# Three chunks per relayout, an earlier w_in and filled TensorE gaps in the first batch of a fused attention and feed-forward kernel

## The chip, the cores and the metric

The kernel runs on one core of a Trainium2 chip. The time is the device time of one execution in microseconds (us). The engines are TensorE (PE; its weight loads are listed apart as PEld), VectorE (DVE), ScalarE (ACT), GpSimd (POOL) and SyncE (SP). SP issues transfers inside the chip and stores, POOL issues the loads that cast float32 to bf16. [...] Results of TensorE are in PSUM, eight banks of 128 x 512 float32.

## The reference

Talking-heads attention followed by a feed-forward part with a squared ReLU, for 8 batches, 12 heads, 448 tokens and head size 64:

```python
scores = scale * np.matmul(q, k.transpose(0, 1, 3, 2))
scores = np.einsum('bhij,hg->bgij', scores, w_pre)
attn = np.exp(scores - np.max(scores, axis=-1, keepdims=True))
attn = attn / (np.sum(attn, axis=-1, keepdims=True) + 1e-09)
attn = np.einsum('bhij,hg->bgij', attn, w_post)
x = np.matmul(attn, v).transpose(0, 2, 1, 3).reshape(B * S, H * D)   # 3584 x 768
h = np.maximum(x @ w_in, 0.0)                                        # 3584 x 2048
out = h * h @ w_out                                                  # 3584 x 768
```

The mixing of heads (w_pre) stands between the scores and the softmax, so all 12 heads of a token have to meet before the maximum is taken.

## The kernel before, in words

**Attention of one batch.** The 448 tokens are four blocks: the last 64 tokens (block r=0, "tail", two heads at a time in 128 rows) and three blocks of 128 rows (r=1 to 3). For each block `score` (L460) multiplies q with k per head (L472), and VectorE or ScalarE copies the result to `snat`, where a row is a query and the heads lie one behind another. There are two `snat` buffers, used in turn by the blocks. Then the layout is changed: `relayout` (L504, its transfer in `move`, L499) takes ten queries of all 12 heads to 120 partitions of a buffer `sch` or `schl`, one row of 448 keys per query and head. That is a chunk. A batch has 45 of them: 6 for r=0 and 13 for each other block, the first of the 13 being made of leftovers of two blocks.

**A chunk** (`chunk`, L552): one product with a 120x120 matrix `wmix` mixes the heads (L564), VectorE takes the minimum (the sign is turned, L569), ScalarE the exponential with its sum (L572), VectorE the reciprocal (L578), POOL scales the second mixing matrix with it into `wq` (L581), four products (L588) give the mixed and transposed weights, and VectorE or ScalarE copies them to `atb` (L302, L304 are the copies of both engines). After 20 chunks `av` (L613, products L624) multiplies half 0 (192 queries) with v, and after the last chunk half 1 (256 queries); the results go to `xt`.

**The feed-forward part** takes two batches together (896 columns) in units of 128, 256, 256 and 256 columns (`UNITS`, `unit`, L649): 96 products with w_in (L669), ReLU on ScalarE (L682), square on POOL (L685), products with w_out (L701), a copy on VectorE (L716) and stores. A unit needs `xt` of its columns; every product of L669 waits for all of w_in, and L701 for w_out.

**The order of the work.** A planner (`Planner`, L76) runs once while the kernel is built. Each operation has an engine, an assumed duration, dependencies, a priority and the PSUM banks it takes. The planner plays the work in time, takes on every engine the ready operation of best priority, and the order that comes out is the fixed order of the instructions on each engine. Chunk n has priority n, its relayout n - 7 (`AHEAD`), FFN work 1e6 and more, so it fills what the attention leaves.

**Loads.** POOL first issues k, the tails of q and q of batch 0, then v. w_in follows in six loads behind the `wq` of chunks 0, 1, 2, 4, 6 and 8 (L776, pieces of 1024 bytes of float32), q and k of batch 1 behind chunks 11 and 14, w_out in four loads behind chunks 17, 20, 23 and 26 (L815). At most seven are under way.

Of the kernel before, what the change touches and what calls it, by code (L numbers as in the profile page):

```python
# [42 lines left out]
AHEAD = 7  # L43
# [4 lines left out]
GROUP = 2  # L48
SLACK = {"PE": 200, "SP": 800, "POOL": 100}
MOST = {"m": 3, "a": 2, "f": 2, "g": 6, "mix": 7}  # L50
PLACES = [[0, 128, 256, 384], [64, 192, 320, 0]]
# [9 lines left out]
UNITS = [(0, 128), (128, 384), (384, 640), (640, 896)]  # L61


class Op:
    def __init__(self, engs, lat, pri, fn, deps, bank, frees, mode):
        self.engs, self.lat, self.pri, self.fn = engs, lat, pri, fn
        self.bank = bank if isinstance(bank, list) else [bank] if bank is not None else []
        self.frees, self.mode = frees, mode
        self.left, self.next, self.at, self.eng, self.ns = 0, [], None, None, 0
        for d in deps:  # L70
            if d is not None:
                self.left += 1
                d.next.append(self)


class Planner:  # L76
# [3 lines left out]
    def __init__(self):  # L80
        self.ops = []
        self.banks, self.most = [], {}

    def add(self, eng, ns, pri, fn, deps=(), lat=60, bank=None, frees=None, mode=0):
        op = Op(eng if isinstance(eng, dict) else {eng: ns}, lat, pri, fn, list(deps), bank, frees, mode)
        self.ops.append(op)
        return op

    def run(self):
# [22 lines left out]
        t, mode = 0, 0  # L112
        while True:
            for eng, heap in ready.items():
                if busy[eng] > t:
                    continue
# [25 lines left out]
                else:  # L142
                    item = None
                    if first is not None:
                        kept.remove(first)
                        item, op, args = first, first[2], []
                if item is not None:
# [21 lines left out]
            while events and events[0][0] == t:  # L169
                op = heapq.heappop(events)[2]  # L170
                if op is None:
                    continue
                if isinstance(op, tuple):
# [14 lines left out]
        assert len(order) == len(self.ops)  # L188
# [4 lines left out]
def kernel(  # L193
# [62 lines left out]

    ident = sb.tile([P, P], BF16, name="ident")
    nc.vector.memset(qt[:, :, :], 0.0)
    for x in range(2):
        load_tail(0, x)  # L260
    for h0 in range(0, H, 4):
        load_kv(ks, k, 0, h0, h0 + 4)
        if h0 == 0:
            masks.make_identity(nc, ident[:, :])
    for h0 in range(0, H, 4):
        load_q(0, h0, h0 + 4)
# [32 lines left out]

    def copy(eng, out_, in_):  # L300
# [20 lines left out]
    def load(nbytes, pri, fn, deps):  # L321
        if len(loads) >= 7:
            deps = list(deps) + [loads[-7]]
        op = add("POOL", 700, pri, fn, deps)
        done = add("LOAD", nbytes / 230.0, len(loads), lambda: None, [op], lat=6000)
# [3 lines left out]
    q_in, k_in, v_in = {}, {}, {}  # L329
    score_ops, scopy = {}, {}  # L330
# [12 lines left out]
    def t_qk(b, p):  # L343
# [27 lines left out]
        at = p - 5 if b == 0 else pri + 3  # L371
# [4 lines left out]
    def t_tail(b, g):  # L376
# [14 lines left out]
        pri = b * NCHUNK - 19 + 3 * g  # L391
# [68 lines left out]
    def score(b, r, p):  # L460
        sn = snat[(b * (NJ + 1) + r) % 2]
        tag = "mfa"[p % 3] if b == 0 and r == 0 else "g"
        group = [p] if r == 0 else range(p, p + GROUP)
        keys = [(tag, "s", b, r, p_, x) for p_ in group for x in range(1 if r == 0 else 2)]

        def mms(*got):
            for key, slot in zip(keys, got):
                _, _, _, _, p_, x = key
# [5 lines left out]
        pri = b * NCHUNK + C0[r] - AHEAD - 0.6 - (0.7 if r == 0 else 1.4) * (NPAIR - p)  # L474
        n = b * (NJ + 1) + r - 2
        old = list(relay_of[n]) if n >= 0 else []
# [15 lines left out]
    ring, side, src_of = [], {}, {}  # L492

# [4 lines left out]
    def move(n, pri, ns, deps, outs, srcs, lat):  # L498
        op = add("SP", ns, pri, lambda: nc.sync.dma_start(out=outs, in_=srcs), deps)  # L499
        done = add("DMA", ns / 2, pri, lambda: None, [op], lat=lat)  # L500
# [3 lines left out]
    def relayout(b, c):  # L504
        r, cc = block_of(c)
        n = b * NCHUNK + c
        blk = b * (NJ + 1) + r
        sn, sn0 = snat[blk % 2], snat[(blk - 1) % 2]
        lat = 5500 if b == 0 and c else 4500
        here = relay_of.setdefault(blk, [])  # L510
        deps = list(scopy[b, r])
        pri = n - AHEAD
        if r == 2 and cc == 0:
            src_of[n] = schl
            here.append(move(n, pri, 700, deps + side.get(b - 1, []), schl[24:96, :], sn[120:126, :, :], lat))
            return
# [12 lines left out]
        for of, r0, r1, srcs in parts:  # L529
            ns = 770 if r1 - r0 > 90 else 500  # L530
            relay_of[of].append(move(n, pri, ns, deps + old, src_of[n][r0:r1, :], srcs, lat))
        if r == 0 and cc == 5:
            here.append(move(
                b * NCHUNK + C0[2], pri + 0.5, 500, deps + side.get(b - 1, []),
# [3 lines left out]
    def places(b, c):  # L538
        r, cc = block_of(c)
        rest, first = (0, NS) if b % 2 else (P_ROWS, 0)  # L540
        if r == 0:
            return [(0, rest + CI * cc, 0, CI)]
# [9 lines left out]
    def chunk(b, c):  # L552
        n = b * NCHUNK + c
# [8 lines left out]

        def f_m(slot):
            nc.tensor.matmul(  # L564
# [30 lines left out]
        def f_ac(eng):  # L595
            for half, x0, s0, w in where:
                copy(
                    eng, atb[half][:, :, :, x0:x0 + w].rearrange("p j g m -> p (j g) m"),
# [3 lines left out]
        m = m_op[n] = add("PE", 190, n, keep(mk, f_m), relay[n] + [at_op.get(n - NE), w_ready], lat=200, bank=mk)  # L602
# [6 lines left out]
        old = [av_op[b - 1, half, g] for half in {u[0] for u in where} for g in range(3)] if b > 0 else []  # L609
# [3 lines left out]
    def av(b, half, g):  # L613
        nx = (XA, XB)[half]
        to = spans(b % 2, half)
        key = ("g", "v", b, half, g)

        def mms(slot):
            v_ = slot[:, :].rearrange("p (a c) -> p a c", a=2)
            for i in range(2):  # L620
                c2 = 2 * g + i
                for jb in range(NB):
                    for hh in range(2):
                        nc.tensor.matmul(  # L624
                            v_[64 * hh:64 * hh + 64, i, 0:nx],
                            lhsT=vs[:, 2 * c2 + hh, jb, :],
                            rhs=atb[half][:, jb, 2 * c2 + hh, :],
# [3 lines left out]
        def evac():  # L631
            v_ = slots[key][:, :].rearrange("p (a c) -> p a c", a=2)
            for c0, x0, w in to:
                nc.scalar.copy(out=xt[:, 2 * g:2 * g + 2, x0:x0 + w], in_=v_[:, :, c0:c0 + w])

        n0 = b * NCHUNK
        cs = range(n0, n0 + C0[2] + 1) if half == 0 else range(n0 + C0[2], n0 + NCHUNK)
        old = []
        if b >= 2:
            for ui, (a, z) in enumerate(UNITS):  # L640
                if any(a < x0 + w and z > x0 for _, x0, w in to):
                    old += h_op[b // 2 - 1, ui]
        pri = cs[-1] + 3
# [240 lines left out]
```

## Time and profile before

| | us |
|---|---|
| median of 3 runs (lowest, highest) | 600.12 (600.09, 600.92) |
| the profiled execution | 599.75 |
| its span, first to last instruction | 598.0 |
| PE, PEld, DVE busy in the span | 562.1, 399.6, 490.7 |
| ACT, POOL busy | 466.8, 321.5 |
| mean granted clock of TensorE | 0.980 |
| first product, first FFN product (L669), first L701 | 8.2, 57.3, 83.0 |
| last product's end | 593.1 |

The table of a stretch gives, for each engine, its busy us and in brackets its instructions, then the clock that TensorE was granted (1.00 is full), the mean busy share of the 16 DMA engines (over 1 when transfers of two queues overlap) and the GB/s. In the chain of waits a line is start, length and what ended last. A busy PE isn't PE at its peak, because a product that runs alone is listed with its latency.

### The profile page before, as it was taken

How to read it: one execution, taken by the hardware profiler on the slowest of the kernel's cores; microseconds unless marked ns; L12 is line 12 of the kernel's file. 1: busy time of each engine (PE TensorE's matmuls, PEld its weight loads, DVE VectorE, ACT ScalarE, POOL GpSimd, SP SyncE). 2: the span in 40 equal slices, each digit the busy share in tenths (PEclk: the TensorE clock that was granted, in tenths of full speed). 3: DMA queues.
4: the chain of work that ended last, by engine and by line, in shares of the span. 5: the costliest groups of instructions: out<-in, count | busy, mean ns of one | idle time of the engine just before them, and what ended most of it. 6: DMA issues, size and time to landing. Idle time of an engine off the chain costs nothing.

```text
span 598.0 us, 16568 instructions
## 1 busy us (share of the span) xinstructions
PE 562.1 (94%) x5517; PEld 399.6 (67%) x5517; DVE 490.7 (82%) x1248; ACT 466.8 (78%) x1220; POOL 321.5 (54%) x587
## 2 busy tenths in 40 slices
PE   4679789999999999999999999999999999999996
PEld 2336656666857766766857867776777857787873
DVE  4888888999798998999798998999798998988011
ACT  2577888888989888988888988898887988888320
POOL 5353718733756527753845727663775724563530
PEclk9867999999999999999999999999999999999999
DMA  9799989974297639956497639984597537321011
GB/s 136 118 227 182 212 143 173 189 157 120 83 190 183 133 101 161 188 131 142 95 178 182 142 97 155 197 148 128 111 197 144 145 97 145 118 91 41 19 54 53
DMA packets 138222, 82.29 MB, mean 138 GB/s; under 512 B 59672, under 2 KB 134680, under 8 KB 138136
## 3 DMA queue, kind: packets, MB, share of 16 engines
q1 hardware_dynamic: 86744, 58.42, 39.4%
q0 software_dynamic: 51392, 22.81, 30.8%
q8 instruction: 43, 0.70, 0.5%
q14 instruction: 43, 0.35, 0.2%
HBM read 45.62 MB, written 11.01 MB: 95 GB/s over the span
## 4 chain that ended last, share of the span: by engine, by line
PE 80%; DVE 8%; issue 3%; ACT 3%; POOL 3%; DMA 3%; SPq 0%; DVEq 0%; ACTq 0%; POOLq 0%
PE bank L669 23%; PE bank L701 23%; PE bank L588 12%; PE bank L564 10%; PE bank L624 6%; PE bank L472 6%; DMA sch<-snat 3%; DVE mn L569 2%; DVE atb L302 2%; ACT es L572 1%; DVE snat L302 1%; POOL wq L581 1%; DVE rc L578 1%; PE bank L355 1%; ACT snat L304 1%
## 5 line engine op out<-in xcount | busy, mean ns | idle before, releaser
L572 ACT ACTIVATE es<-bank,mn 120x448 bf16<-120x448 f32 x360 | 228.2, 641 | 41.9 <-DVE mn L569 34.2
L581 POOL TENSOR_SCALAR wq<-wback,rc 120x120 bf16<-120x120 f32 x360 | 130.5, 366 | 211.6 <-DVE rc L578 132.2
L569 DVE TENSOR_REDUCE mn<-bank 120x1 f32<-120x448 f32 x360 | 208.3, 609 | 4.9 <-PE bank L564 4.7
L701 PE MATMUL bank<-w,h 128*128 128x384 bf16 x896 | 173.4, 325 | 0.3 <-ACT es L572 0.2
L669 PE MATMUL bank<-xt,w 128*128 128x256 bf16 (+1 forms) x1536 | 164.1, 259 | 0.1
L302 DVE CAST atb<-bank 112x480 bf16<-112x480 f32 (+2 forms) x229 | 134.8, 601 | 29.6 <-PE bank L588 27.2
L669 PEld LDWEIGHTS <-w 128*128 128x128 bf16 x1536 | 133.9, 98 | 24.2 <-issue 2.6
L588 PEld LDWEIGHTS <-es 120*112 120x112 bf16 (+1 forms) x1440 | 117.7, 132 | 47.3 <-issue 15.2
L588 PE MATMUL bank<-wq,es 120*112 120x120 bf16 (+1 forms) x1440 | 130.0, 220 | 10.8 <-POOL wq L581 8.8
L685 POOL TENSOR_TENSOR h<-hr 128x512 bf16<-128x512 f32 x112 | 116.3, 1040 | 43.8 <-ACT hr L682 43.4
L701 PEld LDWEIGHTS <-h 128*128 128x128 bf16 x896 | 83.9, 97 | 54.3 <-issue 4.7
L564 PE MATMUL bank<-sch,wmix 120*128 120x448 bf16 x352 | 111.5, 361 | 6.8 <-DMA sch<-snat 2.5
L302 DVE CAST snat<-bank 128x448 bf16<-128x448 f32 x172 | 100.0, 612 | 5.7 <-PE bank L472 3.9
L304 ACT CAST atb<-bank 112x480 bf16<-112x480 f32 (+2 forms) x155 | 85.6, 560 | 16.3 <-PE bank L588 15.5
L682 ACT ACTIVATE hr<-bank 128x512 f32<-128x512 f32 x112 | 67.1, 599 | 32.8 <-PE bank L669 25.3
L304 ACT CAST snat<-bank 128x448 bf16<-128x448 f32 x164 | 81.0, 545 | 13.0 <-PE bank L472 9.8
L572 ACT ACTIVATION_READ_ACCUMULATOR es<-bank,mn 120x1 f32 x360 | 75.2, 209 | 0.0
L578 DVE RECIPROCAL rc<-sm 120x1 f32<-120x1 f32 x360 | 53.0, 153 | 18.9 <-ACT es L572 13.9
L716 DVE COPY osb<-bank 128x384 f32<-128x384 f32 x56 | 30.8, 549 | 35.7 <-PE bank L701 35.5
L564 PEld LDWEIGHTS <-wmix 120*128 120x128 bf16 x360 | 32.1, 98 | 28.0 <-issue 13.5
L472 PE MATMUL bank<-kt,qz 64*128 64x448 bf16 x288 | 43.8, 366 | 2.6 <-DVE qz L302 1.8
L624 PE MATMUL bank<-atb,vs 112*64 112x192 bf16 (+1 forms) x768 | 41.2, 265 | 0.8 <-ACT atb L304 0.6
(45 smaller groups left out, 222.9 us busy)
## 6 DMA issues: line engine op xcount, KB each, us to landing
sch<-snat SPq DMA_DIRECT2D x336, 105.0 KB
out_dram<-osb SPq DMA_DIRECT2D x23, 360.0 KB
vs<-in_v_dram POOLq DMA_DIRECT2D x16, 336.0 KB, 8.9
ks<-in_k_dram POOLq DMA_DIRECT2D x14, 336.0 KB, 9.2
qs<-in_q_dram POOLq DMA_DIRECT2D x14, 288.0 KB, 8.4
w<-in_moe_w_in_dram POOLq DMA_DIRECT2D x6, 512.0 KB, 17.1
w<-in_moe_w_out_dram POOLq DMA_DIRECT2D x4, 768.0 KB, 20.7
out_dram<-osb SPq DMA_DIRECT2D x8, 192.0 KB
```

The lines of the kernel that those rows point to most:

```text
L302: nc.vector.tensor_copy(out=out_, in_=in_)
L304: nc.scalar.copy(out=out_, in_=in_)
L472: nc.tensor.matmul(slot[:, 0:S], lhsT=lhsT, rhs=kt[i][half, :, at_, :], start=True, stop=True)
L564: nc.tensor.matmul(slot[:, 0:S], lhsT=wm[0:rows, :], rhs=src[0:rows, :], start=True, stop=True,)
L569: nc.vector.tensor_reduce(out=mn[i][0:rows, :], in_=slots[mk][0:rows, 0:S], axis=AX.X, op=ALU.min)
L572: nc.scalar.activation(out=es[i][0:rows, 0:S], in_=slots[mk][0:rows, 0:S], func=ACT.Exp, scale=-1.0, bias=mn[i][0:rows, 0:1], accum_out=sm ...
L581: nc.gpsimd.tensor_scalar(out=wq[i][0:rows, :, 0:ns], in0=wback[0:rows, :, 0:ns], scalar1=rc[i][0:rows, 0:1], scalar2=1.0, op0=ALU.mult, o ...
L588: nc.tensor.matmul(slot[0:P_KEYS, jb * H * ns:(jb + 1) * H * ns], lhsT=es[i][0:rows, jb * P_KEYS:(jb + 1) * P_KEYS], rhs=wq[i][0:rows, :, ...
L624: nc.tensor.matmul(v_[64 * hh:64 * hh + 64, i, 0:nx], lhsT=vs[:, 2 * c2 + hh, jb, :], rhs=atb[half][:, jb, 2 * c2 + hh, :], start=(jb == 0 ...
L669: nc.tensor.matmul(slot[:, j * w:(j + 1) * w], lhsT=w1[c2][:, (f0 + j) * 128:(f0 + j + 1) * 128], rhs=xt[:, c2, a:z], start=(c2 == 0), sto ...
L685: nc.gpsimd.tensor_tensor(out=h2_[:, f0:f0 + nf, 0:w], in0=hr[gi % 2][:, :].rearrange("p (f c) -> p f c", f=nf), in1=hr[gi % 2][:, :].rear ...
L701: nc.tensor.matmul(slot[:, 0:384], lhsT=h2_[:, ft, mt * 128:(mt + 1) * 128], rhs=w2[:, ft, nt * 384:(nt + 1) * 384], start=(ft == 0), stop ...
```

## The change

It touches the first batch, and the planner's model of it.

- **Triples.** For r=0 and r=1 of batch 0 (18 chunks, not the leftover chunk of r=1) one transfer moves 60 or 30 queries with three heads per partition: 120 partitions of 3 x 448 elements. Such a buffer holds three chunks. A chunk is mixed from it by three products that add up, each with a 120x128 matrix that has the rows for one of the three heads and the columns of this chunk's ten queries. Before r=2 there are so six triples and three smaller transfers. The five buffers (`tri`) lie in `osb` and `h2`, which the FFN uses later.
- **The matrices.** 18 of them: `pick` (selections of columns of the identity, copied by VectorE) times `wmix` on TensorE, then scaled by a mask (`keep_m`) on VectorE or ScalarE.
- **Order.** The chunks of batch 0 run by `ORDER0`: the tail, the triples of r=1, the leftover chunk of r=1, then r=2 and r=3. The transposes of q follow those of k closely (`Q0`). Scores of batch 0 are taken one pair of heads at a time.
- **AV and units.** AV of batch 0 goes in four pieces (128, 64, 128 and 128 columns), and the units of the first pair are 128, 128, 128, 256 and 256 columns. The first unit follows the leftover chunk of r=1, the second one r=2.
- **Loads.** The first ones are listed as k, both tails, k, k, q, q, q. Right behind them w_in (three loads), v (two), w_in (three), with no wait for a chunk; w_in in pieces of 4096 bytes of float32, which are 2 KB of bf16. q and k of batch 1 are issued at steps 13 and 16, w_out at 18, 21, 24 and 27, now in pieces of 768 columns; every L701 start waits for all of w_out.
- **Dummy products.** From 1.3 us to 130 us of the planner's time, where TensorE would have nothing ready and a bank is free, it puts a product of zeros: 256 columns, taken as 224 ns up to 6 us and as 112 ns after.
- **Model.** Transfers are played as rows on two queues that slow each other; some assumed durations differ. `AHEAD` is 6.8.

The diff, cut to its core:

```diff
-AHEAD = 7
+AHEAD = 6.8
+GROUP_AT = 1
+IDLE_NS, IDLE_COLS, IDLE_END = 112, 256, 130000
+IDLE_COLD, COLD_END, IDLE_FROM = 224, 6000, 1300
+LOADS0 = [("k", 0), ("t", 0), ("t", 1), ("k", 1), ("k", 2), ("q", 0), ("q", 1), ("q", 2)]
+UNITS0 = [(0, 128), (128, 256), (256, 384), (384, 640), (640, 896)]
+TRIPLES = [4 * m + t for t in range(4) for m in range(3)]
+EARLY = 6
+ORDER0 = [
+    *range(EARLY), *[C0[1] + 1 + c for c in TRIPLES], C0[1], *range(EARLY, C0[1]),
+    C0[2], *[C0[2] + 1 + c for c in TRIPLES], C0[3], *[C0[3] + 1 + c for c in TRIPLES],
+]
+W2_AT = [18, 21, 24, 27]
+Q1_AT = [13, 16]
+LAST_W1 = 3
...
+                if item is None and eng == "PE" and free and self.still and IDLE_FROM <= t < IDLE_END:
+                    op = Op({"PE": 0}, 0, 0, self.still, [], None, None, mode)
+                    op.eng, op.ns, op.at = "PE", IDLE_COLD if t < COLD_END else IDLE_NS, t
+                    order.append((op, [free[0], mode]))
+                    busy[eng] = t + op.ns
...
+    still = sb.tile([P, IDLE_COLS], BF16, name="still")
+    nc.vector.memset(still[:, :], 0.0)
...
+    pick = [h2[0][0:KC, f, 0:KC] for f in range(6)]
+    wtri_all = sb.tile([KC, 18, P], BF16, name="wtri_all")
+    wtri = [[wtri_all[:, 3 * m + x, :] for x in range(3)] for m in range(6)]
+    nc.gpsimd.memset(wtri_all[:, :, KC:P], 0.0)
...
+    def spread(tail, slot):
+        for x in range(3):
+            nc.tensor.matmul(
+                slot[0:KC, x * KC:(x + 1) * KC], lhsT=pick[3 * tail + x][:, :], rhs=wmix[1][:, 0:KC], start=True, stop=True,
+            )
+
+    def thin(eng, tail, m, x):
+        src, to = slots["g", "tri", tail][0:KC, x * KC:(x + 1) * KC], wtri[3 * tail + m][x][:, 0:KC]
+        if eng == "DVE":
+            nc.vector.tensor_scalar(out=to, in0=src, scalar1=keep_m[:, m:m + 1], scalar2=1.0, op0=ALU.mult, op1=ALU.mult)
+        else:
+            nc.scalar.activation(out=to, in_=src, func=ACT.Copy, scale=keep_m[:, m:m + 1])
...
+        if triple(b, c):
+            t, m = (cc // 3, cc % 3) if r == 0 else ((cc - 1) % 4, (cc - 1) // 4)
...
+            if m > 0:
+                src_of[n], relay[n] = src_of[n - 1], relay[n - 1]
+                return
+            src_of[n] = tri[len(tris) % NTRI]
+            old = [m_op[tris[-NTRI] + x] for x in range(3)] if len(tris) >= NTRI else []
+            tris.append(n)
+            here.append(move(
+                n, pri, 800, deps + old, src_of[n][:, :, :].rearrange("k x s -> k (x s)"),
+                sn[60 * t:60 * t + 60, 0:NPAIR, :].rearrange("t (g x) s -> t g (x s)", x=3) if r == 0 else
+                sn[t:t + 4 * 29 + 1:4, :, :].rearrange("t (g x) s -> t g (x s)", x=3), lat,
+            ))
+            return
...
         def f_m(slot):
+            if three:
+                for x in range(3):
+                    nc.tensor.matmul(
+                        slot[:, 0:S], lhsT=wtri[sub(b, c)][x][:, :], rhs=src[:, x, :], start=x == 0, stop=x == 2,
+                    )
+                return
...
-                                   [prev] + sq_op[ix] + w2_in[2 * nt:2 * nt + 2], lat=0, bank=key)
+                                   [prev] + sq_op[ix] + w2_in[0:1 if ix < SOON else 4], lat=0, bank=key)
...
-            out=w1[c2][:, :], in_=moe_w_in[c2 * 128:(c2 + 1) * 128, 0:DFF], max_dma_last_dim=1024,
-        ), deps))
+            out=w1[c2][:, :], in_=moe_w_in[c2 * 128:(c2 + 1) * 128, 0:DFF], max_dma_last_dim=4096,
+        ), [started]))
...
+    def first_batch():
+        for i in range(NPAIR):
+            if i == LAST_W1:
+                load_v(0, 0.1 + i, [started])
+            load_w1(i, 0.1 + i)
...
+        for n, c in enumerate(ORDER0):
...
+            if c == C0[1]:
+                for g in range(3):
+                    av(0, 0, g, 0, P_ROWS)
+                unit(0, 0)
+            if c == C0[2]:
+                for g in range(3):
+                    av(0, 0, g, P_ROWS, XA)
+            if c == C0[3]:
+                for g in range(3):
+                    av(0, 1, g, 0, P_ROWS)
+                unit(0, 1)
+        for g in range(3):
+            av(0, 1, g, P_ROWS, XB)
+        unit(0, 2)
...
+    def stand(slot, mode):
+        k_, m_ = P // 2 if mode == ROWS else P, P // 2 if mode == COLS else P
+        nc.tensor.matmul(
+            slot[0:m_, 0:IDLE_COLS], lhsT=still[0:k_, 0:m_], rhs=still[0:k_, :], start=True, stop=True,
+        )
```

## The prediction

> **What bounds the kernel now.** I read the page's slices first, then a table of stretches, then the chain of waits, then the sync engine's issues. In the page each digit is a fortieth of the span, about 15 us.
>
> ```profile
> PE   4679789999999999999999999999999999999996
> DVE  4888888999798998999798998999798998988011
> ACT  2577888888989888988888988898887988888320
> PEclk9867999999999999999999999999999999999999
> ```
>
> TensorE is full except in the first six slices; the second, third and fourth of these (8, 6, 7) are also the only ones with a lowered granted clock. At the end VectorE and ScalarE have nothing to do (digits 0, 1, 1 and 3, 2, 0) and TensorE is still full. So the end is TensorE's total work plus what TensorE lost earlier, and the loss sits in the first batch. The stretches below give busy us of PE, weight loads, DVE, ACT and POOL, then the granted clock, the DMA share and GB/s.
>
> ```profile
> 14.00:24.00 10.00, 6.21 (x65) 2.85 (x63) 9.40 (x25) 6.00 (x15) 2.23 (x4) 1.00 0.54 97
> 24.00:42.00 18.00, 13.63 (x68) 6.33 (x68) 15.31 (x39) 11.81 (x32) 10.15 (x19) 0.53 1.29 206
> ...
> 49.00:55.20 6.20, 5.75 (x48) 4.13 (x49) 5.61 (x15) 5.57 (x17) 2.48 (x7) 0.50 1.03 177
> ...
> 64.00:90.00 26.00, 20.00 (x246) 12.89 (x243) 22.62 (x59) 21.92 (x57) 10.43 (x23) 1.00 1.01 175
> ...
> 140.00:500.00 360.00, 356.67 (x3577) 258.24 (x3576) 323.29 (x817) 308.62 (x815) 207.34 (x381) 1.00 0.72 143
> ```
>
> After 140 us PE is 99% busy, DVE 90% and ACT 86%. From 24 to 42 us PE runs at half clock and shows 68 matmuls. To see what it lost I price its matmuls at the rate of full-clock rows of the chain: 8 of L588 in 0.42 us, 2 of L564 in 0.38, 4 paired L472 in 0.48, 24 of L355 in 0.71, 12 of L669 at 256 columns in 1.31, 24 at 128 columns in 1.34, 4 of L701 in 0.65, 48 of L624 in 2.12 (192 wide) or 2.74 (256 wide). With the counts of the groups, the work done by 57.3 us (the first product of the feed-forward part, FFN) is 20.7 us, by 90 us it is 43.8, and of the whole kernel 525. So PE lost 36.6 us of the first 57.3, 46.2 of the first 90, and only about 22 in the 503 us after.
>
> What holds it there is the chain of a chunk. The chain of waits (start, length, what) and the issues of SP:
>
> ```profile
> 22.69 0.80 SPq L499
> 23.53 0.80 SPq L499
> 24.37 0.91 SPq L499
> 25.33 8.15 DMA sch<-snat
> 33.52 0.55 PE bank L564
> ```
>
> ```profile
> 21.17 13.14 SPq L499 DMA_DIRECT2D sch<-snat  x14
> ```
>
> One relayout per chunk costs SP 0.94 us, and under the w_in loads (issued from 21.9 us, DMA share 1.29) it lands after 8.15 us. The first one, in an idle DMA, went from its issue at 15.45 to its product at 18.56, which is 2.3 us behind its 0.8 us of issue. Two more late things show. L701 of the first FFN unit starts at 83.0 because the second w_out load, issued at 61.6, lands after the group's median of 20.7. Batch 1's second k load, issued at 52.4 with a landing of 21 to 24 us, holds that batch's transposes to 82, and from 84 to 90 us DVE is busy only 3.1 and ACT 3.9 of 6 us.
>
> **The change, part by part.**
>
> *Work added to PE.* 18 chunks get three products for one: 36 x 0.19 = 6.8 us. AV of batch 0 in four widths instead of two doubles its matmuls to 192. At 128 and 64 columns they cost at least the 0.030 us of an L355 transpose, 5.8 us against 4.9, so +0.9. An FFN unit of 256 columns becomes two of 128: 192 x 0.056 against 96 x 0.109, +0.2. The six small products with the pick matrices are 0.1. Sum 8.0 us. The 46.2 us lost before 90 cover it; without that cover it goes to the end in full.
>
> *Set-up.* Twelve copies for the picks at about 0.15 us (rows: smask reduce 0.28, perm copy 0.47), 18 scalings of 120x120 at the 0.22 of a wmix put or 0.3 on ACT, a reduce of 0.28 and small memsets: 6 to 7 us of DVE and ACT. ACT waits 7.0 us idle before 9.05 and is 35% busy from 10 to 20. I take half, 3 us, as falling into a filled stretch. POOL's memset is like ident's 0.22, ahead of wback at 7.72, which the 21.5 us of the first wq covers. The chunk products now also wait for the scaled matrices; behind them stands all of PE, but the data come later (15 us).
>
> *A, the start.* From 8.22 to 15.45 PE's pieces of the chain add to 5.6 us at half rate (two L472 take 0.91 there, 0.24 later). Dummy products from 1.3 us on would warm it: 2.8 us off. Against this, eight loads (w_in, v) now follow q on POOL at about 0.8 us each. POOL has nothing else until 21.5, but their traffic meets the first relayouts: up to +2. I take -1.5 (bounds -2.8, +2). The first FFN product needs w_in at 57 now; earlier is not needed.
>
> *B, 14 to 64 us.* DVE and ACT are busy 42.4 + 35.2 = 77.6 of 100 us. Six triples replace 18 relayouts: SP issues 0.8 for three chunks instead of 2.8, and the bytes are the same. So I expect SP and landing to stop setting the pace, and DVE and ACT to run as in 140 to 500 us (87.8%): (77.6 + 3)/1.755 = 45.9 us, -4.1. Bounds: +1.9 if the share stays at 77.6%; -7.0 at the 93.8% of 64 to 84 us.
>
> *C, 64 to 90 us.* With w_in gone from the queue, batch 1's q and k should land in the 8 to 9 us of the later groups and the hole at 84 closes. At 93.8% the 44.5 us of work take 23.7: -2.3. ScalarE gains four relus of the second unit there, 2.4 us. I take -1.5 (bounds -2.3, +2).
>
> *D, FFN in the gaps.* The second unit (10.5 us) becomes ready after the r=2 chunks, and w_out lands some 20 us sooner, so PE is ahead by up to 10.5 us relative to the attention. How much reaches the end depends on the stock of ready FFN work, which is least near 228 us: then 32 matmuls of L701 remain before a new unit is ready, 5.2 us. I take -5.2 (bounds 0, -10.5).
>
> *E, the dummies.* PE's order is fixed, so a dummy costs nothing while PE waits and 0.11 us when it doesn't. I take 0, the nearest case being the 36.6 us lost in the first 57; bound +6, if PE is late by one contended landing.
>
> **Clock.** The row: from 28 to 32 us PE is busy 3.9 of 4 us with 22 matmuls, yet the granted clock stays 0.50 until 41. By the counts the array streams about 65% of that. The Trainium skill, "TensorE: Matmul & The Clock Gate", section "What you observe" to "What's actually happening", says the clock is 1.2 GHz after an idle window of about 3.4 us and 2.4 GHz after one that is busy. By that rule a plan with filled gaps has no half-rate stretch at all, and the sum would be that of the first rival below. The trace agrees only in part: 0.50 and 1.00 are the two levels, but 4 us that count as busy here did not release it.
>
> **Sum.** -1.5 - 4.1 - 1.5 - 5.2 = -12.3 us. The profiled execution took 599.75 us, 1.75 around its span of 598.0; the median of the runs is 600.12, 0.37 above it. So span 585.7, about 587.8 as a median.
>
> **Rivals.**
> 1. *The attention runs as tight as DVE and ACT allow.* 64 to 84 us at 93.8% speaks for it, the steady 87.8% against. A -2.8, B -7.0, C -2.3, D -5.2: -17.3, 582.8 us.
> 2. *The relayouts weren't the limit.* DVE is at 85% from 14 to 64 us already, and keeps its waits on ACT and PE. Then B is +1.9, C 0, A -1.5, D -5.2: -4.8, 595.3 us.
> 3. *Slower: PE falls behind its fixed order at the first relayouts.* The w_in packets, now 2 KB, stand in the DMA queues when the first triples are issued; these land like the 8.15 us row instead of 2.3, 5.9 late. PE can't make it up, as its slack holds dummies, and the 8.0 us of added work are uncovered: 5.9 + 8.0 - 5.2 = +8.7, 608.8 us. It decides once PE is about 12 us behind at 130 us. Against it: PE waits 18 us by 57 for other reasons. The Trainium skill, "DMA: Bandwidth & Descriptors", section "Queues, rings and completion order", has each DMA engine go round-robin over its queues packet by packet. By that a relayout's share against w_in goes from 896:512 bytes to 2688:2048, which is against the change; no run so far shows it.
> 4. *No change*, gains and added work cancelling (8.0 against A and D).
>
> **Chances and range.** Forecast (584.5 to 592) 0.42; rival 1 0.20; rival 2 0.20; slower 0.14; no change 0.04. A difference under 0.2%, 1.2 us, can't be told from none. Faster is 0.42 + 0.20 + 0.20 = 0.82, same 0.04, slower 0.14. The range 579 to 601 holds the forecast, rival 2, no change and most of rival 1, about 0.82.
>
> **What would show it.** Right: granted clock 1.0 in 8 to 60 us; six relayout issues before the r=2 block; first FFN product near 48 instead of 57; L701 near 62 instead of 83; no hole at 84 to 90; DVE plus ACT near 88% from 14 to 64. Wrong: triples that land after 6 us or more, dummies standing between products whose data are there, or idle PE in the middle batches (then D is spent), in which case the forecast is too low.

## The result and the profile after

The changed kernel takes 602.16 us (median of 20 runs, 599.29 to 606.91) against 600.3 us for the kernel before (20 runs, 599.05 to 602.15). The ratio is 1.0039, interval [1.0023, 1.0056]: slower by 0.4%. That lies outside the range of 579 to 601 us, on the other side of no change. The profiled execution took 600.87 us with a span of 598.8, so the rows below belong to one of its faster executions.

The slices of the page after, to hold against those shown of before:

```profile
PE   6998899999999999999999999999999999999996
DVE  5697878988988998998799897999798898988011
ACT  4597888898999888887888888888988988898420
PEclk9899999999999999999999999999999999999999
```

The gaps of TensorE at the start of its line look filled, and the clock line has a single 8 where it had 8, 6, 7. But filled with what? PE's digits count dummies as well. The lines of VectorE and ScalarE, which do the real work of a chunk, are hardly higher. The stretches after (busy us and instructions of PE, weight loads, DVE, ACT, POOL, then clock, DMA share, GB/s):

```profile
14.00:24.00 10.00, 9.48 (x101) 5.80 (x101) 6.80 (x16) 5.61 (x12) 0.12 (x1) 0.83 1.19 209
24.00:42.00 18.00, 16.75 (x129) 10.04 (x129) 14.93 (x35) 14.30 (x37) 4.34 (x12) 1.00 0.79 186
...
49.00:55.20 6.20, 4.65 (x46) 3.29 (x47) 4.50 (x10) 4.97 (x15) 3.48 (x7) 1.00 1.39 198
64.00:90.00 26.00, 23.25 (x377) 19.05 (x372) 20.65 (x55) 21.95 (x59) 13.06 (x24) 1.00 0.82 175
140.00:500.00 360.00, 356.72 (x3571) 256.88 (x3568) 321.08 (x818) 310.83 (x823) 212.02 (x389) 1.00 0.74 146
```

In 14 to 24 us VectorE is busy 6.8 us where it was 9.4 before, at a DMA share of 1.19 instead of 0.54. From 140 us on nothing has changed. To see what PE really did I price its matmuls at the full-clock durations of the prediction, and set the dummies apart at 0.109 us each. Lost is the rest of the time. The rates are rounded, so the sums are good to about 0.3 us:

| PE by the time given, us | work | dummies | lost |
|---|---|---|---|
| before, by 57.3 | 20.8 | 0 | 36.5 |
| after, by 57.3 | 25.5 | 16.0 | 15.8 |
| before, by 140 | 87.0 | 0 | 53.0 |
| after, by 140 | 94.8 | 23.2 | 22.0 |
| before, 140 to 500 | 346.0 | 0 | 14.0 |
| after, 140 to 500 | 345.1 | 0 | 14.8 |
| before, whole kernel | 525 | 0 | |
| after, whole kernel | 533 | 23.2 | |

Lost time and dummies together fell from 53.0 to 45.2 us by 140. That is 7.8 us, about the 8.0 us of products that the change adds. The forecast needed 8.0 + 12.3 = 20.3.

The transfers that SP issues, after (start, length, count):

```profile
17.38 1.82 SPq L660 DMA_DIRECT2D osb<-snat  x2
...
23.13 2.67 SPq L660 DMA_DIRECT2D h<-snat  x3
26.80 0.85 SPq L660 DMA_DIRECT2D osb<-snat  x1
27.69 1.42 SPq L660 DMA_DIRECT2D sch<-snat  x2
44.44 0.77 SPq L660 DMA_DIRECT2D schl<-snat  x1
45.26 42.33 SPq L660 DMA_DIRECT2D sch<-snat  x32
```

The six triples (osb, h) are there as announced. But the first is issued at 17.38 us (first relayout before: 15.45), and the block of r=2 starts at 45.3 (before: 36.1). The chain of waits after names what holds them:

```profile
7.04 0.35 DVE wtri_all L450
...
13.18 0.34 DVE wtri_all L450
13.53 0.31 DVE kt L397
...
17.38 7.48 DMA osb<-snat
24.91 1.88 PE bank L751 x9
...
27.69 10.75 DMA sch<-snat
...
69.34 16.52 DMA sch<-snat
```

Two things are new at the start. From 7.0 to 13.5 us the scalings of the 18 matrices stand on the chain, in turn on VectorE (10) and ScalarE (8), three times with two in a row on one engine, and a copy of k comes only behind them. Then the first triples take 7.5 us from the issue to the first product, at 24.91. Before, it took 3.1 us and came at 18.56. The timeline shows why the scalings are slow and what waits behind them:

```profile
7.81 0.34 DVE L450 TENSOR_SCALAR wtri_all<-bank,keep_m 120x120 bf16<-120x120 f32 x1 [0.43 <-ACT wtri_all L452]
...
8.18 0.36 ACT L452 ACTIVATE wtri_all<-bank,keep_m 120x120 bf16<-120x120 f32 x1 [0.41 <-DVE wtri_all L450]
8.25 2.19 POOL L990 DMA_DIRECT2D w<-in_moe_w_in_dram  x3
...
8.58 0.34 DVE L450 TENSOR_SCALAR wtri_all<-bank,keep_m 120x120 bf16<-120x120 f32 x1 [0.43 <-ACT wtri_all L452]
...
13.88 0.35 PE L631 MATMUL bank<-kt,zt 128*128 128x448 bf16 x1 [2.73 <-DVE kt L397]
```

Each scaling ends before the other engine's begins (8.15 and 8.18, 8.54 and 8.58), and the brackets name the other engine's scaling as what the wait was for. All nine scalings of a group read one PSUM bank. That this is the reason is argued, not shown, since no run spreads the results over two banks. That both write one buffer, `wtri_all`, isn't enough: from 20.85 us both engines write one `snat` buffer at the same time, each from banks of its own. The 18 take 6.5 us. The score product at 13.88 has waited 2.73 us for the copy of k behind them. And at 8.25 us, in the same lines, w_in is issued: its six loads stand ahead of the first triples, and land after a median of 15.8 us.

### The profile page after: what moved, and what is told of

It reads as the page before. It is cut to its first block, busy times and chain, and to the rows that moved or that the text cites. A ratio compares the mean times of both kernels' runs of the same rounds, so it can differ in the third digit from the quotient of the medians.

```text
span 598.8 us, 17463 instructions
## 1 busy us (share of the span) xinstructions
PE 580.2 (97%) x5964; PEld 418.7 (70%) x5964; DVE 487.6 (81%) x1250; ACT 477.6 (80%) x1250; POOL 322.9 (54%) x591
## 4 chain that ended last, share of the span: by engine, by line
PE 86%; DMA 8%; ACT 2%; DVE 2%; issue 1%; SPq 1%; POOL 0%; DVEq 0%; ACTq 0%
PE bank L904 24%; PE bank L872 24%; PE bank L779 12%; PE bank L755 11%; PE bank L819 6%; DMA sch<-snat 6%; PE bank L631 6%; PE bank L1101 2%; DMA osb<-snat 1%; ACT es L763 1%; ACT snat L399 1%; DVE wtri_all L450 1%; SPq L660 1%; DVE snat L397 1%; ACT wtri_all L452 0%
## 5 line engine op out<-in xcount | busy, mean ns | idle before, releaser
L772 POOL TENSOR_SCALAR wq<-wback,rc 120x120 bf16<-120x120 f32 x360 | 132.2, 371 | 211.2 <-DVE rc L769 132.2
L904 PE MATMUL bank<-w,h 128*128 128x384 bf16 x896 | 173.2, 325 | 0.1
L397 DVE CAST atb<-bank 112x480 bf16<-112x480 f32 (+3 forms) x213 | 131.0, 627 | 23.2 <-PE bank L779 20.9
L779 PEld LDWEIGHTS <-es 120*112 120x112 bf16 (+1 forms) x1440 | 114.6, 129 | 35.3 <-issue 8.2
L779 PE MATMUL bank<-wq,es 120*112 120x120 bf16 (+1 forms) x1440 | 127.7, 217 | 1.1 <-POOL wq L772 0.4
L904 PEld LDWEIGHTS <-h 128*128 128x128 bf16 x896 | 84.1, 97 | 53.9 <-issue 3.3
L397 DVE CAST snat<-bank 128x448 bf16<-128x448 f32 x174 | 101.7, 613 | 12.9 <-PE bank L631 5.8
L755 PE MATMUL bank<-sch,wmix 120*128 120x448 bf16 x334 | 104.1, 353 | 5.1 <-DMA sch<-snat 4.3
L399 ACT CAST atb<-bank 112x480 bf16<-112x480 f32 (+3 forms) x171 | 91.7, 550 | 16.5 <-PE bank L779 15.5
L755 PEld LDWEIGHTS <-wmix 120*128 120x128 bf16 x342 | 30.3, 98 | 20.0 <-issue 10.9
L819 PE MATMUL bank<-atb,vs 112*64 112x192 bf16 (+3 forms) x864 | 40.8, 250 | 0.0
## 6 DMA issues: line engine op xcount, KB each, us to landing
w<-in_moe_w_in_dram POOLq DMA_DIRECT2D x6, 512.0 KB, 15.8
```

What stands on the lines that cost most here:

```text
L397: nc.vector.tensor_copy(out=out_, in_=in_)
L399: nc.scalar.copy(out=out_, in_=in_)
L755: nc.tensor.matmul(slot[:, 0:S], lhsT=wm[0:rows, :], rhs=src[0:rows, :], start=True, stop=True,)
L772: nc.gpsimd.tensor_scalar(out=wq[i][0:rows, :, 0:ns], in0=wback[0:rows, :, 0:ns], scalar1=rc[i][0:rows, 0:1], scalar2=1.0, op0=ALU.mult, o ...
L779: nc.tensor.matmul(slot[0:P_KEYS, jb * H * ns:(jb + 1) * H * ns], lhsT=es[i][0:rows, jb * P_KEYS:(jb + 1) * P_KEYS], rhs=wq[i][0:rows, :, ...
L819: nc.tensor.matmul(v_[64 * hh:64 * hh + 64, i, 0:x1 - x0], lhsT=vs[:, 2 * c2 + hh, jb, :], rhs=atb[half][:, jb, 2 * c2 + hh, x0:x1], start ...
```

## The experiments

Theories at first: **T1**, the start costs that the change brings itself (w_in ahead of the triples, the scalings in turn) eat the gain; **T2**, the dummies cost time; **T3**, three products per chunk cost more than the relayouts saved. Later: **T4**, the leftover chunk's late transfer keeps a buffer of scores occupied and so delays r=2; **T5**, the loads of batch 1 and w_out hold the relayouts of r=2; **T6**, the start doesn't reach the end (it comes with e9). In the first eight kernels the planner made a new order from the edited input (e5 excepted); in the others every engine keeps the order of the changed kernel, but for the instructions named.

**e1, no dummies** (re-planned).

```diff
-    pl.still = stand
+    pl.still = None
```

> The changed kernel without its dummy products (221 of 256 columns, 24 us of TensorE at full clock). Theory T1: the time is set by late relayouts in the first batch (second scalings ahead of the k copies, and w_in queued ahead of the first triples), and the dummies only fill waits: within 2 us of the changed kernel (600 to 604), granted clock about 0.5 again in parts of 14 to 60 us. Rival T2: the dummies hold up real products in the fixed order: 590 to 597, and the attention at 75 us at least 4 chunks further.

Measured 600.75 us, ratio to before 1.0006 [0.998, 1.0032]. That is in T1's range and far from T2's. By 75 us 37 chunks were through their minimum, against 36 after, where T2 needed four more. The interval overlaps that of after, and the order is a new one.

**e2, w_in behind the wq of chunks 0, 1, 2, 4, 6 and 8 again** (re-planned).

```diff
+W1_AT = [0, 1, 2, 4, 6, 8]
...
-            load_w1(i, 0.1 + i)
...
+            if W1_AT is not None and n in W1_AT:
+                load_w1(W1_AT.index(n), n, gate(n))
```

> The changed kernel with w_in issued behind the wq of steps 0, 1, 2, 4, 6 and 8 as in the kernel before, still in 2 KB packets. T1: the first triple lands in 2.5 to 4 us instead of 7.5, the first chunk product comes at 19 to 21 us instead of 24.9, the r=2 scores start before 36 instead of 39, the attention is 4 chunks further at 75 us: 592 to 597 us. T2: the first products come earlier too, but the end moves by less than 1.5 us. A third theory, T3 (the added 6.8 us of triple products): less than 1.5 us as well.

Measured 610.43 us, 1.0179 [1.0125, 1.0232]: much slower, against T1. But the first triples now took 4.75 us from issue to product (18.64 to 23.39), not 7.5; the product came 1.5 us sooner, less than T1 had it. The loss came in the middle, where this row stands against 356.72 for PE after:

```profile
140.00:500.00 360.00, 350.55 (x3429) 249.62 (x3427) 316.74 (x810) 306.61 (x807) 206.63 (x382) 0.99 0.72 143
```

By full-rate prices PE lost 25.7 us in these 360 us, against 14.8 after. Nothing was edited there; the new order differs there too.

**e3, the second nine scalings at a later priority** (re-planned).

```diff
-        at_pri = -30 if tail else -17
+        at_pri = -30 if tail else -6
```

> The changed kernel with the second nine scalings (those for r=1) at a later priority, -6 instead of -17, so that they stand behind the copies of k. T1: the first score of the second pair group no longer waits for k from 11.1 to 13.9 us, the first relayout is issued 1.5 to 2 us earlier than 17.4, but it still meets w_in: 599.5 to 602. T2 and T3: no difference over 1 us.

Measured 606.18 us, 1.0095 [1.0059, 1.0132]. The first triple was issued at 17.03 and used at 24.97, so almost nothing of the start was gained.

**e4, no triples** (single relayouts and one product in r=0 and r=1, no matrices; re-planned).

```diff
-TRI_IN = (0, 1)
+TRI_IN = ()
...
-    for tail in (1, 0):
+    for tail in () if not TRI_IN else (1, 0):
```

> The changed kernel with one relayout and one product per chunk again (no triples, no pick matrices and no scalings), all else as changed: w_in early, dummies, units, order. T1: 18 relayouts behind w_in take longer than six triples, while the 2 us of scalings and the 6.8 us of products go: between 598 and 606 us. T3: the triple products are what costs: 592 to 596 us.

Measured 618.01 us, 1.0295 [1.0242, 1.0347]. SP's lines show the old chain of single transfers, and r=2 starting ten us later than after:

```profile
13.66 4.91 SPq L660 DMA_DIRECT2D sch<-snat  x6
...
19.43 20.02 SPq L660 DMA_DIRECT2D sch<-snat  x14
54.34 0.75 SPq L660 DMA_DIRECT2D schl<-snat  x1
```

This speaks against T3: the rest of the change without the triples is 16 us worse (618.01 against 602.16). But a new order is part of that: some 9 of the 16 us were lost from 140 to 500 us, where nothing was edited. What the triples are worth by themselves isn't shown.

**e5, dummies planned and not sent** (the order is the same).

```diff
-    pl.still = stand
+    pl.still = lambda slot, mode: None
```

> The changed kernel with exactly its order of instructions, in which the dummies are planned but not sent, so that only their execution is missing. If the dummies hold up real products (T2): 2 to 6 us faster than the changed kernel's 602.2. If they only fill waits and the full clock they give is of use: 0 to 2 us slower. By the first run without dummies (600.75, with another order) I expect 600 to 602.

Measured 603.21 us, 1.0047 [1.0021, 1.0073]. After is 1.0039 [1.0023, 1.0056]. T2's gain didn't come, as in e1, and neither a cost nor a use of the dummies can be told from the noise. The traces show why both may cancel at the start. In the changed kernel the first 16 transposes of k start at 5.92 us, right behind 24 dummies, and take 0.58 us. Here they start at 5.59, when k has landed, and take 0.96.

**e6, the leftover chunk's relayout ahead of r=1** (re-planned).

```diff
-        pri = n - AHEAD
+        pri = (EARLY - 0.5 if b == 0 and r == 1 and cc == 0 else n) - AHEAD
```

> The changed kernel with the relayout of the leftover chunk of r=1 issued ahead of the triples of r=1 instead of behind them. Theory T4: the scores of r=2 need the snat buffer of r=0, which is free only when this relayout has landed; it is issued at 27.7 and lands at 38.4, so r=2's relayouts begin at 45 instead of 36. Then here r=2's relayouts begin at 36 to 40, the attention is 3 to 5 chunks further at 60 us, 595 to 599 us. If T4 is wrong: r=2's relayouts still begin after 43 and the time is within 2 us of 602.

Measured 613.26 us, 1.021 [1.0157, 1.0264]. The relayouts of r=2 still began at 43.2 us, and PE lost 27.4 us in 140 to 500. The first triple, too, was issued 1.4 us later than after (18.75), so this order is no clean test of T4.

**e7, all scalings on ScalarE** (re-planned).

```diff
-                    {"DVE": 220, "ACT": 300}, 0, at_pri + 0.1 * m, lambda eng, tail=tail, m=m, x=x: thin(eng, tail, m, x), [mm],
+                    "ACT", 360, at_pri + 0.1 * m, lambda eng="ACT", tail=tail, m=m, x=x: thin(eng, tail, m, x), [mm],
```

> The changed kernel with all 18 scalings on ScalarE. In the changed kernel they alternate strictly between VectorE and ScalarE, 0.36 us each, from 7.0 to 13.5 us, because they read one PSUM bank; the k copies stand among them. Here the copies of k run on VectorE beside the scalings: first relayout issued at 15 to 16 instead of 17.4. T1: 600 to 602, since the first triples still meet w_in. If the start sets the end one to one: 599 to 600.5.

Measured 603.46 us, 1.0063 [1.0036, 1.009]. The first triple was issued at 15.28 instead of 17.38, but was used at 23.27: 8 us behind w_in.

**e8, the loads of batch 1 and w_out earlier** (re-planned).

```diff
-W2_AT = [18, 21, 24, 27]
+W2_AT = [9, 11, 13, 15]
-Q1_AT = [13, 16]
+Q1_AT = [5, 7]
```

> The changed kernel with batch 1's q and k issued at steps 5 and 7 instead of 13 and 16, and w_out at 9, 11, 13, 15 instead of 18 to 27. In the changed kernel the DMA engines idle from 38 to 46 us and are full from 48 to 74, with r=2's and r=3's relayouts among the loads. If that clash sets the attention's pace (T5): L904 starts near 75 instead of 100, the attention is 3 chunks further at 80 us, 595 to 599 us. If T4 holds instead, r=2's relayouts still start at 45 and the time moves by less than 2 us.

Measured 602.94 us, 1.0049 [1.0026, 1.0072]; r=2 from 43.9 us, L904 from 101.7. No gain, against T5.

After eight kernels the start had moved part of the way that T1 said (e2, e7), but the end hadn't. In e2, e3 and e6 it had moved the other way, by 4 to 11 us. So I stopped the planner from answering: the next kernels take its finished order, and only move or exchange the instructions named.

**e9, e2's edit with the order kept.**

```diff
+        w1_ops.append(pl.ops[-2])
...
+        held, behind = [], [wq_op[n] for n in (0, 1, 2, 4, 6, 8)]
         for op, args in pl.run():
+            if op in w1_ops:
+                held.append((op, args))
+                continue
             op.fn(*args)
+            if op in behind:
+                op, args = held.pop(0)
+                op.fn(*args)
```

`w1_ops` are the six loads of w_in.

> The changed kernel with its planned order kept on every engine, except that POOL issues the six w_in loads behind the wq of steps 0, 1, 2, 4, 6 and 8. A new order from the planner, which made the earlier runs hard to read (PE lost 26 us from 140 to 500 us in the run with w_in gated, 15 in the changed kernel), is so ruled out. Theory T1 (w_in ahead of the first triples sets the time): first triple lands in 4 to 5 us, 2 to 4 us faster than the changed kernel, 598 to 600. Theory T6 (the start doesn't reach the end, since VectorE and ScalarE are full from 28 to 52 us and the later relayouts clash with loads in any case): within 1.5 us of 602.

Measured 598.8 us, 0.9972 [0.9951, 0.9993]: T1's time, and not T6's. The first product came at 23.29, 5.95 us behind the issue at 17.34. The same edit in e2 gave 610.43: 11.6 us between two orders.

**e10, e7's edit with the order kept.**

```diff
-        if eng == "DVE":
+        if eng == "none":
```

No scaling meets this condition any more, so all 18 go to ScalarE.

> The changed kernel with its order kept, and all 18 scalings on ScalarE, so that VectorE has only the k copies there. First relayout at 15.3 to 16.5 instead of 17.4. T1: 1 to 2 us faster than the changed kernel, 600 to 601. T6: within 1 us of 602.

Measured 600.18 us, 0.9993 [0.9975, 1.0011]. Issue at 14.96, first product at 22.69: 7.7 us, still behind w_in. The time is T1's, not T6's.

**e11, both edits of e9 and e10.**

> Both edits with the order kept. T1: first chunk product at 19 to 21 us instead of 24.9 and 4 to 6 us off the end, 596 to 598. T6: less than 2 us, 600 to 603.

Measured 594.99 us, 0.9897 [0.9878, 0.9916]. This is the decisive run: below T1's range, far below T6's, and faster than before. The timeline of e11: the 18 scalings run as one block on one engine, and VectorE copies k among them.

```profile
7.77 4.64 ACT L452 ACTIVATE wtri_all<-bank,keep_m 120x120 bf16<-120x120 f32 x18
...
10.36 0.39 DVE L397 COPY kt<-bank 128x448 bf16<-128x448 bf16 x1 [1.39 <-PE bank L493]
```

One engine alone needs 4.64 us, two in turn needed 6.5. SP's issues in e11 and the stretches that changed:

```profile
15.94 1.83 SPq L660 DMA_DIRECT2D osb<-snat  x2
...
41.00 42.51 SPq L660 DMA_DIRECT2D sch<-snat  x32
```

```profile
14.00:24.00 10.00, 9.86 (x100) 6.30 (x100) 7.37 (x18) 6.34 (x16) 0.28 (x1) 1.00 0.56 135
24.00:42.00 18.00, 17.56 (x145) 10.24 (x143) 17.04 (x41) 16.43 (x43) 10.32 (x22) 1.00 1.08 214
```

The DMA share of 14 to 24 is back at 0.56. The first product comes at 20.92, 5.0 us behind the issue. It wasn't the data that it waited for. On the chain it stands right behind 15 dummies:

```profile
19.35 1.64 PE bank L1102 x15
20.98 0.69 PE bank L751 x3
```

From 24 to 42 us VectorE is busy 17.0 of 18 us (after: 14.9), POOL 10.3 (after: 4.3). r=2 starts 4.3 us sooner. PE's work by 140 us is 98.5 us (after: 94.8), lost and dummies 41.5 (45.2).

**e12, as e11, with w_in behind chunks 5 to 10.**

```diff
-        held, behind = [], [wq_op[n] for n in (0, 1, 2, 4, 6, 8)]
+        held, behind = [], [wq_op[n] for n in (5, 6, 7, 8, 9, 10)]
```

> Both edits, with w_in behind the wq of steps 5 to 10, so that it uses the stretch from 36 to 46 us, in which the DMA engines are idle in the changed kernel, and meets neither the triples nor the leftover. T1: r=2's relayouts begin at 38 to 41 instead of 45, but w_in lands at 55 to 60 and holds the first FFN product to about 60, as now: 595 to 599. T6: 600 to 603; slower, 603 to 606, if w_in lands later than 62 and the FFN has to wait.

Measured 594.6 us, 0.9908 [0.9891, 0.9926]: as e11. The relayouts of r=2 begin at 40.5 us and the first FFN product comes at 57.7.

The forecast's last 7 us were still missing, so four more kernels start from e12.

**e13, the leftover's two transfers ahead of the triples of r=1 on SP.**

```diff
...
+        plan = pl.run()
+        moved = [i for i, (op, _) in enumerate(plan) if op in left_ops]
+        at = min(i for i, (op, _) in enumerate(plan) if op in r1_ops)
+        plan = plan[:at] + [plan[i] for i in moved] + [x for i, x in enumerate(plan) if i >= at and i not in moved]
```

> The fastest version so far (order kept, scalings on ScalarE, w_in behind steps 5 to 10; 594.6) with SP issuing the two transfers of the leftover chunk ahead of the four triples of r=1; the order of all other engines is kept. T4 (r=2's scores wait until the leftover has left the snat buffer): r=2's relayouts start at 36 to 38 instead of 40.5 and 1 to 3 us come off the end. If the order on VectorE and ScalarE, and not the buffer, holds the r=2 copies: no change over 1 us, or 1 us slower, since the triples are issued 1.6 us later.

Measured 595.37 us, 0.9926 [0.99, 0.9952]. The leftover's transfers were issued at 18.06 us, and those of r=2 still at 40.1 (e12: 40.5). T4 fell for this version. In the changed kernel itself the chain does have r=2's first copy (38.78) behind the leftover's landing (38.44).

**e14, the four loads of w_out behind chunks 28, 32, 36 and 40**, held and released as w_in in e9.

```diff
+        held2, behind2 = [], [wq_op[n] for n in (28, 32, 36, 40)]
...
```

> The same version with w_out issued behind the wq of steps 28, 32, 36 and 40 instead of 18 to 27, the order else kept. L904 starts at about 100 us and doesn't need w_out sooner, while its four loads (18 us each, issued at 47 to 65) run among the relayouts of r=2 and r=3. T5 (this clash slows the attention): 2 to 3 chunks further at 80 us, 592 to 594. If the clash costs nothing: 594 to 595.5; slower if L904 has to wait.

Measured 593.7 us, 0.9914 [0.9885, 0.9943]. From 64 to 84 us PE is busy as in e12 and VectorE and ScalarE a little more (16.97 and 18.64, e12 16.36 and 18.44); by 90 us 48 chunks were through their minimum, in e12 45. But the profiled execution is the fastest of five (591.43 us) and had issued its first triple 1.1 us sooner than e12's (14.80 against 15.90), long before the first w_out load. The interval covers e12's ratio, so T5 stays open.

**e15, e12 with the dummies planned and not sent** (e5's diff).

> The same version with its dummies planned but not sent. In the changed kernel this made no clear difference (603.2 against 602.2). If the dummies hold up PE once the relayouts are in time: 592 to 594. If the full clock is of use: 595 to 598.

Measured 596.46 us, 0.9937 [0.9909, 0.9965]. The granted clock fell to 0.50 in 49 to 55 us, and yet the intervals of e12 and e15 overlap; between the ratios themselves lie 0.29%, 1.7 us. In e11, whose dummies are those of e12, they make up 16.8% of the chain in the first 100 us. A chain names what ran last; a dummy that is taken away leaves a wait in its place. Here the first chunk product waits 1.91 us for its data and comes at 19.43, 4.3 us behind the issue; in e12 it came at 20.88, right behind 15 dummies.

**e16, both edits of e13 and e14.**

> Both the leftover first and w_out later. If T4 and T5 hold: 590 to 592. If neither: 594 to 596.

Measured 594.73 us, 0.992 [0.9889, 0.9952]. Nothing added to e14.

So e11 to e14 and e16 end 0.7 to 1.0% below before. Which of them is best can't be told: e12's ratio lies in the intervals of all the others.

## Why the prediction was wrong

**The bound.** Right: the end is PE's work plus what PE lost early. In the ten kernels with one order the end follows the lost time: lost and dummies by 140 us are 46.9 in e10, 45.2 after, 44.2 in e9, 41.5 in e11 and 38.0 in e14, with spans of 599.1, 598.8, 598.0, 593.5 and 589.6. In all ten the span less this time lies between 550 and 554 us.

**Added work.** Right: 533 - 525 = 8.0 us, as summed. The sum put these 8.0 us at nothing, as covered by lost time. They were covered, but the lost time shrank by no more than that (7.8), so nothing was left for the forecast gain.

**Step A failed, and it decides the sign.** The prediction put the start at -1.5 us: -2.8 for the clock, up to +2 for w_in's traffic, and nothing for the set-up. Measured at the first chunk product it is +6.3 (24.91 against 18.56): 1.9 from the later issue and 4.4 from the longer way to the product. Triples that land after 6 us or more were one of the prediction's own signs of being wrong. Three terms were mis-sized:

- *w_in ahead of the triples.* Late w_in alone is worth 1.0039 - 0.9972 = 0.67%, 4.0 us at the end (e9). The time from issue to product fell from 7.5 us to 5.95 in e9 and 5.0 in e11. e9 keeps the 2 KB packets, so the 4.0 us belong to the early issue; the packets weren't tested by themselves. The prediction's rival 3 had this mechanism, a landing like the 8.15 us row, and priced it at 5.9 at the place. Its second half, that PE can't make it up because its slack holds dummies, isn't borne out: without dummies the end can't be told from that of after (e5).
- *The set-up.* It was costed at 0.22 and 0.3 us per scaling, 3 us of it in step B, and none in step A, since the data were to come later anyway. The scalings took 0.34 and 0.36 each (two in a row 0.59 to 0.61) and one after the other, 6.5 us on the path, with copies of k behind them. The prediction added up busy times of two engines as if they ran beside each other, and didn't ask which bank both read. Without it: 1.0039 - 0.9993 = 0.46%, 2.8 us (e10).
- *The clock.* Its 2.8 us can't be found. Among the kernels with all scalings on ScalarE and w_in late, the first triple is issued at 15.17 us without dummies (e15) and at 14.80 to 15.94 with them (e11 to e14, e16).

Both together are 1.0039 - 0.9897 = 1.42%, 8.5 us (e11), more than the sum of 6.8. By the intervals each of the three is good to some 1.6 us. What one edit is worth rests on the medians alone, since the profiled executions of after, e9 and e10 lie within 1.1 us of each other; for both edits the traces show it too. Without the scalings in turn the triples only run into w_in sooner (e10's 7.7 us); this fits, but the intervals are too wide to show it.

**Step B failed.** SP and the landing of the relayouts were to stop setting the pace, and VectorE and ScalarE to be busy 87.8% of 14 to 64 us. Before, after and e11:

```profile
14.00:64.00 50.00, 39.61 (x359) 23.97 (x357) 42.42 (x109) 35.15 (x97) 23.64 (x44) 0.76 1.08 177
14.00:64.00 50.00, 46.68 (x523) 30.71 (x522) 39.08 (x95) 38.05 (x98) 16.55 (x36) 0.97 0.96 179
14.00:64.00 50.00, 48.12 (x551) 32.64 (x551) 40.52 (x100) 39.42 (x104) 23.28 (x46) 0.97 1.03 192
```

After, they were 39.08 + 38.05 = 77.1 of 100 us, no more than the 77.6 before, as rival 2 had it. SP issues less often, as forecast, but the landing still sets the pace: of the chain of the first 100 us, transfers out of `snat` make up 15.0% before, 42.4% after and 22.0% in e11. The late start lies in this window too, so after can't part A from B; e11 does so better, with 79.9%. By the prediction's formula (80.6 us of work over twice the share) 79.9% gives 50.4 us, +0.4 instead of -4.1. That is 4.5 of the 6.3 us between e11's 594.1 (0.9897 x 600.3) and the forecast. What holds VectorE and ScalarE back in e11 isn't settled: neither an earlier leftover (e13) nor later w_out loads (e14) moved the end beyond the noise. That the copies of r=2's scores come late by the fixed order is a guess that fits e13's issues; no run tests it.

**Step C failed, in part.** From 84 to 90 us VectorE and ScalarE are now busy 4.3 and 5.1 of 6 (3.1 and 3.9 before), so the hole is smaller. But 64 to 84 fell from 93.8% to (16.33 + 16.81) / 40 = 82.9%:

```profile
64.00:84.00 20.00, 14.65 (x189) 9.17 (x186) 19.53 (x53) 17.98 (x48) 9.53 (x21) 1.00 1.10 182
64.00:84.00 20.00, 17.81 (x299) 14.55 (x293) 16.33 (x44) 16.81 (x47) 8.68 (x18) 1.00 0.89 178
```

On the chain a relayout of 16.5 us stands there, from 69.34, behind batch 1's q and k (issued 45 to 51) and w_out (51 to 67). The hole moved more than it closed.

**Step D didn't come.** The first FFN product comes at 59.7 us, not near 48 (before: 57.3). The first product with w_out (L904) starts at 100.0 us, not near 62 (L701 before: 83.0), and in e11 at 96.4. The order puts it there; the data no longer do: in e14, which issues its last w_out load at 81.5 us instead of 63.9, it starts at 92.9. How much FFN work done early is worth at the end remains untested.

**Step E and the clock.** The 0 for the dummies is as near as the runs tell, but by luck in part. They were to cost nothing because PE waits anyway. Yet in e9, e11, e12 and e14 the first chunk product stands right behind 15 of them, and the first transposes of k start right behind 24, at 6.30 us in e12; without dummies they start at 5.35 (e15). The granted clock was 1.0 but for 14 to 24 us (0.83). The stretches at 0.53 and 0.50 of before are gone, and that alone brought nothing that the intervals show: without dummies e5 ends 0.08% and e15 0.29% above their fellows. The first rival, which a full clock was to bring, fell with step B. The Trainium skill, "TensorE: Matmul & The Clock Gate", section "What's actually happening", has 1.2 GHz behind an idle window of about 3.4 us. Here 0.50 was granted at 16 to 18 us, though the longest wait of PE before it was 2.73 us.

**What stays open.** Some 6 us of the forecast, what the triples are worth by themselves, and what the two edits of the best kernels would do under an order planned for them.

## What to carry to other kernels

Ask of every set-up step which bank it reads, and add up as one queue what two engines do on one bank. A load that is taken out of a crowded stretch goes somewhere: price it where it lands, here at the first transfers of the start. When a planner orders the whole kernel, keep its order fixed to test a cause, since with one and the same edit two orders lay 11.6 us apart (e2 and e9).

## What the runs showed of the hardware

- *18 scalings out of one PSUM bank at a time were slower on two engines than on one.* In turn they took 6.5 us (0.34 and 0.36 each and some 0.03 between them), on ScalarE alone 4.64 us. The Trainium skill, "PSUM — Partial Sum Buffer", section "PSUM bank collisions raise a hardware error", says that two engines mustn't touch one bank and quadrant in the same cycle and that software has to keep them apart. The timeline agrees: none of the scalings shown overlap.
- *Landing.* The first triples (2688 bytes per partition) took 7.5 us to the product behind w_in in 2 KB packets, 5.0 with w_in later (e11, where dummies held the product), and 4.3 with neither w_in nor dummies ahead (e15).
- *A lowered clock in the first batch isn't seen at the end.* e15 was granted 0.50 in 49 to 55 us, 0.73 in 55 to 64 and 0.81 to 0.83 in 14 to 24 and 42 to 49, and its interval overlaps that of e12, which had 0.84 or more in all of these.
- *Spread.* The runs of after lie between 599.29 and 606.91 us, those of before between 599.05 and 602.15; no run explains it. One part varies at the very start: with one order, the 24 dummies ahead of the first transposes took 4.12 us (e16) to 5.30 us (e12).
